# Token step and first inverse step on eight small PE tiles, W fetched once, front reordered

## The chip, the core and the metric

The kernel runs on one core of a Trainium2 chip. The metric is device microseconds of one execution. The engines are PE (TensorE; its weight loads are shown apart as PEld), VectorE (DVE), ScalarE (ACT), GpSimd (POOL) and SyncE (SP), which issues nearly all DMAs.

## The reference

A spectral filter `a` and a diagonal state-space model `b` work on the same `x` (2048 tokens x 1024 features, bf16), and a gate mixes them per token.

```python
X = rfft2(x); X = X * (w_r + 1j * w_i); a = irfft2(X)       # over tokens and features
Lam_bar = exp(dt * Lam)
Bu = x @ B_bar.T                                            # complex, 1024 states
h[t] = Lam_bar * h[t-1] + Bu[t]                             # 2048 steps
b = 2 * real(h @ C.T) + x * Dskip
g = sigmoid((x * gate_w).sum(-1))
out = g * a + (1 - g) * b
```

## The kernel before

**Two strands.** The model strand works through eight chunks of 256 tokens. `unit(c, q)` makes Bu for one chunk and half of the states: two halves (real, imaginary) of 32 matmuls each (L319), with a ScalarE eviction each (L321). `recur` cuts the recurrence of the chunk into pieces for VectorE: products with tables of cosine and sine (L274, L277), joins, scans (L289), and the way back. `early(tb)` multiplies a tile of 128 tokens of h by C (L598, L602) for tiles 0 to 9 and parks the result in DRAM; tiles 10 to 15 are finished in the tail by `own_tile`, and `late_tile` fetches the parked ones.

The spectral strand is a 2D transform by matrix products. The feature step `fd` (L359, L362) works on rows of tokens turned by PE (`turn_x`, L684) and folded by VectorE (`fold`). Then come the first token step `s1` (L376, two tiles of 64 rows side by side), a turn through DRAM (`turn1_dram`, written at L383), the second token step `s2` (L488, a 32-point transform), the product with W (`times_w`, L496 and L497), the first inverse step `is1` (L512, L513, 64-point), a second turn through DRAM, the second inverse step `is2` (L537), and in the tail the inverse feature step (`spectral`, L629).

**s2, product and is1 before.** There are 16 groups of two columns `b`. For a group, `s2` runs two matmuls of 128x128 weights over 512 columns; the 128 rows of weights hold a block structure in which half of the entries are zero (two interleaved 32-point transforms). Its output rows hold real parts in the upper 64 and imaginary parts in the lower 64, so each half of the partitions needs the same W: it is fetched twice, with four DMAs for a group.

```python
for r in range(2):
    nc.sync.dma_start(out=Wb[g % 3][64 * r:64 * (r + 1), w, :, 1:K], in_=W_v[w][:, bs, 1:K])
```

`times_w` makes two products, X2 with the imaginary and with the real part of W. `is1` adds two matmuls of 128x128 weights for each of the two columns. The buffers `psA` are two PSUM tiles of 128x1024 FP32 that all spectral steps share; `psU` has two more, for the model strand.

**Order.** PE, VectorE and ScalarE run in the order in which the program is written; the DMAs of SP and POOL are placed by the framework's scheduler. In the front (until `tctx.close()`), a table `plan` says for each of 16 rows in which order `turn_x` (T), `fold` (f), `fd` (F) and `s1` (S) are issued, and `order` which loads follow: B by DMA transposes (`load_B`, L218), C (`load_C`, L583), tables. Small vectors for the recurrence (L869 to L903) stand in one run after row 5. The tables of cosine and sine (`make_tab`) and halves of the model strand fill in between. After the front the spectral strand is a generator, `gfnet`, which `step()` moves on; between its steps stand halves of the model strand (`halves(ssm, 1)`) and pieces of VectorE's work. `vector(next(share))` issues pieces up to an amount of estimated microseconds from the list `SHARE`.

Group g+3 of `s2`'s input is loaded after `is1` of group g; the 16 groups have one half of the model strand each.

Of the kernel before, what the change touches and what calls it, by code (L numbers as in the profile page):

```python
# [19 lines left out]
S = 2048  # L20
D = 1024
# [24 lines left out]
def _host_consts():  # L46
# [14 lines left out]
    for cls in range(2):  # L61
        for kb in range(2):
# [10 lines left out]
    m1 = np.arange(64)[None, None, :]  # L73
# [8 lines left out]
    f = np.arange(P)  # L82
    fs, fr, fa = f[:, None] // 4, (f[:, None] // 2) % 2, f[:, None] % 2
    hr, hm, ha = f[None, :] // 64, (f[None, :] // 2) % 32, f[None, :] % 2
    angF = 2 * np.pi * ((fs * hm) % 32) / 32
    K2 = (fa == ha) * np.where(fr == hr, np.cos(angF), np.where(fr == 1, 1.0, -1.0) * np.sin(angF))
    pp = (np.arange(P) % 64)[:, None, None]
    bb = np.arange(32)[None, :, None]
    nn = np.arange(64)[None, None, :]
    angM = 2 * np.pi * (((32 * pp + bb) * nn) % S) / S  # L90
    top = (np.arange(P) < 64)[:, None, None]
    Mre = np.where(top, np.cos(angM), -np.sin(angM))
    Mim = np.where(top, np.sin(angM), np.cos(angM))
    gr, gb, ga = f // 64, (f // 2) % 32, f % 2
    angR = 2 * np.pi * ((gb[:, None] * gb[None, :]) % 32) / 32
    R2 = (ga[:, None] == ga[None, :]) * np.where(gr[:, None] == gr[None, :], np.cos(angR),
                                                  np.where(gr[:, None] == 0, 1.0, -1.0) * np.sin(angR))
    R2 = R2.reshape(P, 64, 2).transpose(0, 2, 1).reshape(P, P)
    Sel = np.zeros((P, 2, 2, P))
    for h in range(2):  # L100
        for ri in range(2):
            Sel[2 * np.arange(64) + h, h, ri, 64 * ri + np.arange(64)] = 1.0
# [11 lines left out]
        MT=b16(np.concatenate([-Mim, Mre, Mim], axis=2)),  # L114
        KRS=b16(np.concatenate([K2, R2, Sel.reshape(P, 4 * P)], axis=1)),
# [5 lines left out]
def kernel(  # L121
# [29 lines left out]
    W_v = [w.rearrange("(p b) k -> p b k", b=32) for w in (A_w_r, A_w_i)]  # L151
# [27 lines left out]
    psX = xctx.enter_context(tc.tile_pool(name="psX", bufs=2, space=PSUM, reuse_waits="tile"))  # L179
# [85 lines left out]
    def recur(c, js, home):  # L265
# [21 lines left out]
        def scan(ri, j):  # L287
            seg = u[:, ri, j:j + 4].rearrange("p j t -> p (j t)")
            nc.vector.tensor_tensor_scan(out=seg, data0=rz[:, js.start + j:js.start + j + 4].rearrange("p j t -> p (j t)"),  # L289
                                         data1=seg, initial=0.0, op0=ALU.mult, op1=ALU.add)  # L290
# [14 lines left out]
        t = 0.15 + 0.27 * n  # L305
        both = lambda f, g: lambda: (f(), g())
        pieces = [(t, lambda: cross(1)), (t, lambda: along(0)), (t / 2 + 0.1, join_re), (t / 2 + 0.3, join_im)]
        pieces += [(2.3, lambda ri=ri, j=j: scan(ri, j)) for j in range(0, n, 4) for ri in range(2)]
# [40 lines left out]
    def gfnet():  # L349
# [4 lines left out]
        def fd(j):  # L354
# [9 lines left out]
            X1 = gta.tile([P, 2, K], BF16, name="X1")  # L364
            (nc.vector.tensor_copy if j in (3, 5) else nc.scalar.copy)(  # L365
# [4 lines left out]
        def s1(j):  # L370
# [10 lines left out]
            (nc.vector.tensor_copy if j in (0, 1, 2, 3, 5, 6, 7) else nc.scalar.copy)(out=A1, in_=psa)  # L381
# [14 lines left out]
        MT_sb = raw.rearrange("p (b n) -> p b n", n=192)  # L396
# [5 lines left out]
        t1_v = turn1_dram.rearrange("j (r a b) k -> (j r a) b k", r=2, a=2)  # L402
        Wb = fft["Wb"]

        def load(g):
            bs = slice(2 * g, 2 * g + 2)
            Bb = gt.tile([P, 2, K], BF16, name="Bb", tag="gin", bufs=3)
            nc.sync.dma_start(out=Bb, in_=t1_v[:, bs])
            for w in range(2):
                for r in range(2):  # L410
                    nc.sync.dma_start(out=Wb[g % 3][64 * r:64 * (r + 1), w, :, 1:K], in_=W_v[w][:, bs, 1:K])  # L411
            return Bb

# [22 lines left out]
        loads = [load(0), load(1), load(2)]  # L436
# [4 lines left out]
        nc.vector.tensor_copy(out=Bcol[:, 0:2].rearrange("j c a b -> j (c a b)"), in_=aps)  # L441
# [34 lines left out]
        qps = psA.tile([P, 2, 16], FP32, name="qps", tag="ps")  # L476
        for h in range(2):
            for ri in range(2):
                nc.tensor.matmul(qps[:, h, :], lhsT=fft["Sel"][:, 2 * h + ri, :], rhs=Qb[:, :, ri],
                                 start=(ri == 0), stop=(ri == 1))  # L480
        Qn = fx.tile([P, 2, 16], BF16, name="Qn")
        nc.vector.tensor_copy(out=Qn, in_=qps)
        Qn = Qn.rearrange("p h b -> p (h b)")

        def s2(g):
            ps2 = psA.tile([P, 2, K], FP32, name="ps_s2", tag="ps")
            for h in range(2):
                nc.tensor.matmul(ps2[:, h, :], lhsT=KRS_sb[:, 0, :], rhs=loads[g][:, h, :], start=True, stop=True)  # L488
            X2 = gt.tile([P, 2, K], BF16, name="X2", tag="gev", bufs=3)
            nc.scalar.copy(out=X2, in_=ps2)  # L490
            nc.scalar.copy(out=X2[:, :, 0], in_=Qn[:, 2 * g:2 * g + 2])
            return X2

        def times_w(g, X2):
            V2 = gt.tile([P, 2, K], BF16, name="V2", tag="gv2", bufs=2)
            nc.vector.tensor_mul(out=V2, in0=X2, in1=Wb[g % 3][:, 1])  # L496
            nc.vector.tensor_mul(out=X2, in0=X2, in1=Wb[g % 3][:, 0])  # L497
            return X2, V2

        yield "qn"  # L500
        X2s = [s2(0)]
        yield "s2"
        X2s.append(s2(1))
        UV = times_w(0, X2s.pop(0))
        yield "uv"
        for g in range(16):
            if g + 2 < 16:
                X2s.append(s2(g + 2))
            psc = psA.tile([P, 2, K], FP32, name="ps_is1", tag="ps")
            for h in range(2):  # L510
                b = 2 * g + h
                nc.tensor.matmul(psc[:, h, :], lhsT=MT_sb[:, b, 64:192], rhs=UV[0][:, h, :], start=True, stop=False)  # L512
                nc.tensor.matmul(psc[:, h, :], lhsT=MT_sb[:, b, 0:128], rhs=UV[1][:, h, :], start=False, stop=True)  # L513
            C1 = gt.tile([P, 2, K], BF16, name="C1", tag="gc1", bufs=2)
            nc.scalar.copy(out=C1.rearrange("p h (c i) -> p h c i", c=2), in_=psc.rearrange("p h (i c) -> p h c i", c=2))  # L515
            nc.sync.dma_start(out=turn2_dram[2 * g:2 * g + 2].rearrange("b m k -> m b k"), in_=C1)
            yield "is1"
            if g + 1 < 16:
                UV = times_w(g + 1, X2s.pop(0))
            if g + 3 < 16:  # L520
                loads.append(load(g + 3))
            yield "uv"
        yield "ib"
        ZT = fft["ZT"].rearrange("p i t (h u) -> p i (t h) u", h=2)
        t2_v = turn2_dram.rearrange("b (r G a g) k -> G r b a g k", r=2, a=2, g=4)

        for G in range(8):
            Cq = raw[:, 2 * D * (G % 3):2 * D * (G % 3 + 1)].rearrange("p (g k) -> p g k", g=4)
            for r in range(2):
                nc.sync.dma_start(out=Cq[64 * r:64 * (r + 1)], in_=t2_v[G, r])  # L530
            for kp in range(2):
                psz = psA.tile([P, 2, K], FP32, name="ps_is2", tag="ps")
                for kl in range(2):
                    kc = 2 * kp + kl
                    pv = psz[:, kl, :].rearrange("p (a g n) -> p a g n", a=2, g=4)
                    for g in range(4):
                        nc.tensor.matmul(pv[:, :, g, :], lhsT=Cq[:, g, P * kc:P * (kc + 1)], rhs=KRS_sb[:, 1, :],  # L537
                                         start=True, stop=True)
                nc.scalar.copy(out=ZT[:, 4 * kp:4 * kp + 4, :, 8 * G:8 * G + 8].rearrange("p (c r) n t -> p c r n t", c=2),  # L539
                               in_=psz.rearrange("p c (t r n) -> p c r n t", t=8, r=2))  # L540
                yield "is2"

    def after_ia():
# [10 lines left out]
        fft["Sel"] = fft["gt"].tile([P, 4, P], BF16, name="Sel_sb", tag="gc1", bufs=2)  # L554
        nc.sync.dma_start(out=fft["Sel"], in_=cKRS.rearrange("p (i m) -> p i m", m=P)[:, 2:6])
        fft["Wb"] = [fft["wp"].tile([P, 2, 2, K], BF16, name=f"Wb{i}") for i in range(3)]
# [203 lines left out]
    fft["KRS"] = fx.tile([P, 2, P], BF16, name="KRS_sb")  # L760

    def load_small():
        nc.sync.dma_start(out=fft["JP"], in_=cJP)
        nc.sync.dma_start(out=fft["KRS"], in_=cKRS.rearrange("p (i m) -> p i m", m=P)[:, 0:2])
# [26 lines left out]
    def halves(gen, n):  # L791
# [5 lines left out]
    order = {  # L797
        1: [(load_B, 4)],
        2: [(load_B, 2)],
# [65 lines left out]
    for _ in range(5):  # L865
        front()
# [145 lines left out]
```

## Time and profile before

| | |
|---|---|
| median of 3 runs | 337.9 us (337.06 to 338.51) |
| profiled execution | 338.71 us, span 336.9 us |
| mean granted clock of PE | 0.995 |
| PE busy | 323.7 us (96%), 2446 matmuls |
| VectorE busy | 286.7 us (85%) |
| ScalarE busy | 169.3 us (50%) |
| DMA | 58.45 MB, mean 173 GB/s |
| first matmul of s2, last of s2 | 122.7 us, 191.0 us |
| first matmul of is2 | 211.7 us |

A busy time is the union of an engine's instructions; matmuls overlap, so their mean length (379 ns for 512 columns) is more than the time each holds the engine. Times inside the span count from its start.

### The profile page before, as it was taken

How to read it: one execution, taken by the hardware profiler on the slowest of the kernel's cores; microseconds unless marked ns; L12 is line 12 of the kernel's file. 1: busy time of each engine (PE TensorE's matmuls, PEld its weight loads, DVE VectorE, ACT ScalarE, POOL GpSimd, SP SyncE). 2: the span in 40 equal slices, each digit the busy share in tenths (PEclk: the TensorE clock that was granted, in tenths of full speed). 3: DMA queues.
4: the chain of work that ended last, by engine and by line, in shares of the span. 5: the costliest groups of instructions: out<-in, count | busy, mean ns of one | idle time of the engine just before them, and what ended most of it. 6: DMA issues, size and time to landing. Idle time of an engine off the chain costs nothing.

```text
span 336.9 us, 6192 instructions
## 1 busy us (share of the span) xinstructions
PE 323.7 (96%) x2446; PEld 213.7 (63%) x2446; DVE 286.7 (85%) x403; ACT 169.3 (50%) x213; POOL 32.4 (10%) x64
## 2 busy tenths in 40 slices
PE   8998859999999999999999999999999999999995
PEld 4564636676885675747566576869845876565552
DVE  2798895899979789999999999899680999999951
ACT  3888679746351155647556551646632243443510
POOL 1481112020000000000000000000000002211220
PEclk9999989999999999999999999999999999999999
DMA  7999999999992447889999956997214003776594
GB/s 265 378 175 227 204 211 208 164 172 218 272 220 55 115 135 175 251 192 284 261 253 252 232 163 170 216 195 203 70 28 136 19 0 53 109 159 89 98 156 154
DMA packets 83581, 58.45 MB, mean 173 GB/s; under 512 B 54328, under 2 KB 74304, under 8 KB 83424
## 3 DMA queue, kind: packets, MB, share of 16 engines
q1 hardware_dynamic: 80304, 55.38, 66.8%
q0 software_dynamic: 3168, 2.66, 8.7%
q8 instruction: 19, 0.31, 0.4%
q14 instruction: 10, 0.08, 0.1%
q10 hardware_dynamic: 80, 0.01, 0.0%
HBM read 30.23 MB, written 17.83 MB: 143 GB/s over the span
## 4 chain that ended last, share of the span: by engine, by line
PE 83%; ACT 5%; DVE 5%; SPq 4%; issue 1%; DMA 1%; ACTq 0%; DVEq 0%
PE ps_y L598 29%; PE psu L319 28%; PE ps_h L598 4%; PE ps_id L629 4%; SPq L583 3%; PE ps_fd L359 2%; PE ps_is L537 2%; PE ps_is L513 2%; PE ps_is L512 2%; PE ps_s L488 2%; PE ps_y L602 2%; PE pt L684 2%; PE psw L710 1%; ACT xQ L685 1%; SPq L411 1%
## 5 line engine op out<-in xcount | busy, mean ns | idle before, releaser
L319 PE MATMUL psu<-xQ,BT 128*128 128x256 bf16 x1024 | 117.9, 275 | 0.8 <-ACT ye L616 0.5
L319 PEld LDWEIGHTS <-BT 128*128 128x128 bf16 x1024 | 100.1, 99 | 17.4 <-issue 3.2
L598 PE MATMUL ps_y<-CT,h 128*128 128x512 bf16 x448 | 101.3, 379 | 0.0
L598 PEld LDWEIGHTS <-h 128*128 128x128 bf16 x512 | 49.4, 98 | 55.4
L289 DVE TENSOR_TENSOR_SCAN h<-rz,h 128x1024 bf16<-128x1024 f32 x32 | 71.5, 2274 | 0.1
L321 ACT CAST h<-psu 128x1024 bf16<-128x1024 f32 x32 | 32.3, 1010 | 52.5 <-PE psu L319 49.2
L277 DVE TENSOR_TENSOR h<-h,tab 128x4096 bf16<-128x4096 bf16 (+1 forms) x20 | 37.3, 1863 | 0.7
L644 POOL DMA_DIRECT2D BT<-y_scratch x10 | 11.9, 1194 | 235.4 <-DVE BT L638 235.1
L616 ACT ACTIVATE ye<-ps_y,omg 128x512 f32<-128x512 f32 x20 | 12.7, 684 | 43.4 <-PE ps_y L602 35.7
L274 DVE TENSOR_TENSOR xQ<-h,tab 128x4096 bf16<-128x4096 bf16 x12 | 27.4, 2287 | 4.4 <-ACT h L321 4.3
L490 ACT CAST X<-ps_s 128x1024 bf16<-128x1024 f32 x16 | 16.2, 1014 | 8.7 <-PE ps_s L488 8.7
L359 PE MATMUL ps_fd<-G_sb,preT 128*128 128x512 bf16 x64 | 16.5, 380 | 1.2 <-ACT X L365 1.2
L685 ACT COPY xQ<-pt 128x1024 bf16<-128x1024 bf16 x16 | 15.4, 1024 | 2.5 <-PE pt L684 2.5
L539 ACT CAST ZT<-ps_is 128x1024 bf16<-128x1024 f32 x16 | 15.5, 1023 | 2.2 <-PE ps_is L537 2.2
L695 DVE TENSOR_TENSOR preT<-xQ 128x512 bf16<-128x512 bf16 x16 | 7.3, 453 | 10.9 <-ACT xQ L685 7.6
L515 ACT CAST C<-ps_is 128x1024 bf16<-128x1024 f32 x16 | 16.1, 1008 | 0.0
L629 PE MATMUL ps_id<-raw,ZT 128*128 128x256 bf16 x128 | 15.9, 273 | 0.0
L365 ACT CAST X<-ps_fd 128x1024 bf16<-128x1024 f32 x14 | 14.2, 1013 | 3.0 <-PE ps_fd L362 2.9
L376 PE MATMUL ps_s<-X,raw 64*128 64x512 bf16 x64 | 9.7, 380 | 5.1 <-DVE CT L381 4.5
L598 PE MATMUL ps_h<-CT,h 128*128 128x512 bf16 x64 | 14.5, 379 | 0.0
L629 PEld LDWEIGHTS <-ZT 128*128 128x128 bf16 x128 | 12.4, 98 | 2.2
L496 DVE TENSOR_TENSOR V<-X,Wb 128x1024 bf16<-128x1024 bf16 x16 | 10.9, 680 | 1.6 <-issue 1.5
(194 smaller groups left out, 367.9 us busy)
## 6 DMA issues: line engine op xcount, KB each, us to landing
y_scratch<-ye SPq DMA_DIRECT2D x20, 256.0 KB, 2.6
CT<-in_A_x_dram SPq DMA_DIRECT2D x8, 512.0 KB, 5.4
Bb<-turn_scratch SPq DMA_DIRECT2D x16, 256.0 KB, 4.0
turn_scratch<-C SPq DMA_DIRECT2D x16, 256.0 KB, 5.1
raw<-turn_scratch SPq DMA_DIRECT2D x16, 256.0 KB, 4.5
Wb<-in_A_w_r_dram SPq DMA_DIRECT2D x32, 127.8 KB, 4.1
Wb<-in_A_w_i_dram SPq DMA_DIRECT2D x32, 127.8 KB, 3.8
out_dram<-BT SPq DMA_DIRECT2D x14, 256.0 KB, 5.2
```

Source lines behind the costliest of these rows:

```text
L274: nc.vector.tensor_mul(out=tmps["s"], in0=u[:, ::-1], in1=bc(i))
L277: nc.vector.tensor_mul(out=u, in0=u, in1=bc(i))
L289: nc.vector.tensor_tensor_scan(out=seg, data0=rz[:, js.start + j:js.start + j + 4].rearrange("p j t -> p (j t)"), data1=seg, initial=0.0, ...
L319: nc.tensor.matmul(psu[:, j, :], lhsT=BT[4 * q + j][:, ri, d8, :], rhs=xQ[:, c, d8, :], start=(d8 == 0), stop=(d8 == 7))
L321: nc.scalar.copy(out=hs[c][:, ri, 4 * q:4 * q + 4].rearrange("p b (q j) -> p b q j", j=32), in_=psu.rearrange("p b (j q) -> p b q j", j=32))
L359: nc.tensor.matmul(ps[:, 1, :], lhsT=preTs[j][:, 4 + d4, :], rhs=Go[:, d4, :], start=(d4 == 0), stop=(d4 == 3))
L490: nc.scalar.copy(out=X2, in_=ps2)
L515: nc.scalar.copy(out=C1.rearrange("p h (c i) -> p h c i", c=2), in_=psc.rearrange("p h (i c) -> p h c i", c=2))
L539: nc.scalar.copy(out=ZT[:, 4 * kp:4 * kp + 4, :, 8 * G:8 * G + 8].rearrange("p (c r) n t -> p c r n t", c=2), in_=psz.rearrange("p c (t r ...
L598: nc.tensor.matmul(psy, lhsT=hs[c][:, ri, jb, P * tq:P * (tq + 1)], rhs=CT[ri][:, jb, 512 * dh:512 * (dh + 1)], start=(i == 0), stop=False)
L629: nc.tensor.matmul(pse[:, slot, :], lhsT=ZT_t[:, i, tb, :], rhs=fft["Gi"][:, i, :], start=(kb == 0), stop=(kb == 1))
L685: nc.scalar.copy(out=x_gjq[:, :, :, :, j, :].rearrange("p c d g q -> p d c g q"), in_=pt.rearrange("p d (c q g) -> p d c g q", c=NCH, g=2))
```

## The change

The two steps use tiles of the PE array that are as large as their blocks. `s2` has 8 groups; a group holds two sets of 64 rows (b) and four columns (c), and for the real and the imaginary output (r) it issues eight matmuls of 64 rows by 32 columns. So real and imaginary parts lie side by side in the free dimension, and all 128 partitions hold different values of the token index. `is1` has four accumulating passes of eight matmuls of 32 rows by 64 columns. W is fetched once, for four columns at a time and two groups (`load_W`; two buffers, one of them in `raw`, where the smaller table `MT` leaves room). A product takes both parts of W at once, with X2 spread over the two parts of W and W spread over the two parts of X2.

```diff
+        def load_W(i):
+            pair, w = i // 2, i % 2
+            for c in range(4):
+                nc.sync.dma_start(out=Wb[pair % 2][32 * c:32 * (c + 1), w, :, 1:K], in_=W_v[w][c][:, 4 * pair:4 * pair + 4, 1:K])
...
         def s2(g):
-            ps2 = psA.tile([P, 2, K], FP32, name="ps_s2", tag="ps")
-            for h in range(2):
-                nc.tensor.matmul(ps2[:, h, :], lhsT=KRS_sb[:, 0, :], rhs=loads[g][:, h, :], start=True, stop=True)
-            X2 = gt.tile([P, 2, K], BF16, name="X2", tag="gev", bufs=3)
-            nc.scalar.copy(out=X2, in_=ps2)
-            nc.scalar.copy(out=X2[:, :, 0], in_=Qn[:, 2 * g:2 * g + 2])
+            ps2 = [psA.tile([P, 2, K], FP32, name="ps_s2", tag="ps") for _ in range(2)]
+            for r in range(2):
+                for c in range(4):
+                    for b in range(2):
+                        nc.tensor.matmul(ps2[b][32 * c:32 * (c + 1), r, :], lhsT=KRS_sb[64 * b:64 * (b + 1), 0, 32 * r:32 * (r + 1)],
+                                         rhs=loads[g][64 * b:64 * (b + 1), c, :], start=True, stop=True, tile_position=(64 * b, 32 * c))
+            X2 = []
+            for b in range(2):
+                X2.append(gt.tile([P, 2, K], BF16, name="X2", tag="gev", bufs=2))
+                nc.scalar.copy(out=X2[b], in_=ps2[b])
+                nc.scalar.copy(out=X2[b][:, :, 0], in_=Qn[:, 2 * g + b, :])
...
-            nc.vector.tensor_mul(out=V2, in0=X2, in1=Wb[g % 3][:, 1])
-            nc.vector.tensor_mul(out=X2, in0=X2, in1=Wb[g % 3][:, 0])
+                nc.vector.tensor_mul(out=UV[b], in0=X2[b].unsqueeze(1).to_broadcast([P, 2, 2, K]),
+                                     in1=Wb[g // 2 % 2][:, :, at:at + 1, :].to_broadcast([P, 2, 2, K]))
...
-                nc.tensor.matmul(psc[:, h, :], lhsT=MT_sb[:, b, 64:192], rhs=UV[0][:, h, :], start=True, stop=False)
-                nc.tensor.matmul(psc[:, h, :], lhsT=MT_sb[:, b, 0:128], rhs=UV[1][:, h, :], start=False, stop=True)
+            psc = [psA.tile([P, 2, K], FP32, name="ps_is1", tag="ps") for _ in range(2)]
+            for i, (u, r, n) in enumerate(((0, 0, 64), (0, 1, 32), (1, 0, 32), (1, 1, 0))):
+                for c in range(4):
+                    rows = slice(32 * c, 32 * (c + 1))
+                    for b in range(2):
+                        nc.tensor.matmul(psc[c // 2][64 * b:64 * (b + 1), c % 2, :], lhsT=MT_sb[rows, 2 * g + b, n:n + 64],
+                                         rhs=UV[b][rows, u, r, :], start=(i == 0), stop=(i == 3), tile_position=(32 * c, 64 * b))
```

The reads and writes of the two turns through DRAM follow the new index order (the read for `is2` is one DMA for a group instead of two); `is2` keeps its 128 matmuls of 128x128. `qps` is one matmul instead of four.

The order of the whole program up to the tail is now one string, `ORDER`, with a letter for each act: T, f, F, S as above, h a half of the model strand, v a share of VectorE's pieces, t a part of a cosine table, a a part of the small vectors (now the generator `small`), b one B transpose, c a part of C, s a step of the spectral strand, w and k loads, g the gate.

```diff
+ORDER = (
+    "FTfSTbTTFSbfTbfbTTFfTTSfbbFbTbfbTwSTSFf2TTbaFfSabaxatfbbFbhtSttt",
+    "fFftbbSthttFShStttfthfFkttFtvttthtStvgfFcFtStShtvtcvttchtttSFtth",
+    "tttvFcSttttSt|cvvcsccdhvhvvehvshhvshhvvshvhvshvsshvshvsshvshvssh",
+    "vsvhshsvshvsshshvsvshvshvsshvsvhsshvshvshvhvhvsvshvsvshvsvshsvvs",
+    "hvsvvshsvshvsivshvsvsvh",
+)
-    psX = xctx.enter_context(tc.tile_pool(name="psX", bufs=2, space=PSUM, reuse_waits="tile"))
+    psX = xctx.enter_context(tc.tile_pool(name="psX", bufs=4, space=PSUM, reuse_waits="tile"))
-        pieces += [(2.3, lambda ri=ri, j=j: scan(ri, j)) for j in range(0, n, 4) for ri in range(2)]
+        pieces += [(2.3 * m / 4, lambda ri=ri, j=j: scan(ri, j, m)) for j in range(0, n, m) for ri in range(2)]
-            X1 = gta.tile([P, 2, K], BF16, name="X1")
-            (nc.vector.tensor_copy if j in (3, 5) else nc.scalar.copy)(
+            X1 = gta.tile([P, 2, K], BF16, name="X1", bufs=4)
+            (nc.vector.tensor_copy if j in (0, 3, 5, 10, 15) else nc.scalar.copy)(
-            (nc.vector.tensor_copy if j in (0, 1, 2, 3, 5, 6, 7) else nc.scalar.copy)(out=A1, in_=psa)
+            (nc.vector.tensor_copy if j in (0, 1, 3, 5, 6, 9) else nc.scalar.copy)(out=A1, in_=psa)
```

In `ORDER`, `s2` of a group and `is1` of the group before alternate, with one half of the model strand between each two. Of the eight c, four stand in the front, two before the step `w` (which issues the first loads of `s2`'s input and of W), and two after it. `SHARE` has new values; up to the last half ahead of the tail they sum to 160.7 in place of 154.6. A scan now runs over all eight blocks of a chunk at once where `recur` has the whole chunk.

More of the change, by code (lines that the diff above doesn't have):

```diff
@@ L435, in gfnet @@
         nc.vector.tensor_scalar_mul(out=beta, in0=beta, scalar1=0.25)
-        loads = [load(0), load(1), load(2)]
+        loads = [load(0), load(1)]
+        for i in range(4):
+            load_W(i)
         yield "w"
@@ L475, in gfnet @@
         yield "q"
[L476 to L483, printed above, removed]
-        def s2(g):
-            ps2 = psA.tile([P, 2, K], FP32, name="ps_s2", tag="ps")
-            for h in range(2):
-                nc.tensor.matmul(ps2[:, h, :], lhsT=KRS_sb[:, 0, :], rhs=loads[g][:, h, :], start=True, stop=True)
-            X2 = gt.tile([P, 2, K], BF16, name="X2", tag="gev", bufs=3)
-            nc.scalar.copy(out=X2, in_=ps2)
-            nc.scalar.copy(out=X2[:, :, 0], in_=Qn[:, 2 * g:2 * g + 2])
+        qps = psA.tile([P, 32], FP32, name="qps", tag="ps")
@@ new lines, in gfnet @@
+        nc.tensor.matmul(qps, lhsT=KRS_sb[:, 2, :], rhs=Qb.rearrange("p b r -> p (b r)"), start=True, stop=True)
+        Qn = fx.tile([P, 16, 2], BF16, name="Qn")
+        nc.vector.tensor_copy(out=Qn.rearrange("p b r -> p (b r)"), in_=qps)
+        def s2(g):
+            ps2 = [psA.tile([P, 2, K], FP32, name="ps_s2", tag="ps") for _ in range(2)]
[9 more added lines that the diff above has]
+                nc.scalar.copy(out=X2[b][:, :, 0], in_=Qn[:, 2 * g + b, :])
@@ L876 @@
-    xctx.close()
-    pools["u"] = ctx.enter_context(tc.tile_pool(name="psU", bufs=2, space=PSUM, reuse_waits="tile"))
-    for _ in turns:
-        pass
     sth, cth = s2c[:, 0], c2c[:, 0]
-    sTC = sp.tile([P, 8], FP32, name="sTC"); nc.vector.tensor_mul(out=sTC, in0=s2c[:, 1], in1=r_sb)
-    cTC = sp.tile([P, 8], FP32, name="cTC"); nc.vector.tensor_mul(out=cTC, in0=c2c[:, 1], in1=r_sb)
+    sTC = sp.tile([P, 8], FP32, name="sTC")
+    cTC = sp.tile([P, 8], FP32, name="cTC")
     rot = sp.tile([P, 2, 2, 8], FP32, name="rot")
-    nc.vector.tensor_copy(out=rot[:, 0, 1], in_=sTC)
@@ L917 @@
-    tctx.close()
-    for q in range(4, 8):
-        load_C(q)
-    for v, n in (("w", 4), ("a", 1), ("z", 2), ("q", 2), ("qn", 1), ("s2", 0), ("uv", 1)):
-        assert step() == v
-        for i in range(n):
-            if v == "w" and i == 0:
-                nc.vector.tensor_mul(out=fft["dgD"], in0=ident.unsqueeze(1).to_broadcast([P, 8, P]),
-                                     in1=vecT[:, 3].unsqueeze(2).to_broadcast([P, 8, P]))
-            if v == "w" and i == 3:
-                gate_end()
-            halves(ssm, 1)
-            vector(next(share))
@@ L930 @@
-    for g in range(16):
-        assert step() == "is1"
-        assert step() == "uv"
-        halves(ssm, 1)
-        vector(next(share))
-    halves(ssm, 1)
-    vector(next(share))
-    halves(ssm, 1)
-    vector(next(share))
-    for g in range(16):
-        assert step() == "is2"
-        if g == 12:
-            after_ic()
-        if g % 2:
-            halves(ssm, 1)
-        vector(next(share))
+    lbr = sp.tile([P, 8], FP32, name="lbr")
+    lbi = sp.tile([P, 8], FP32, name="lbi")
+    nr = sp.tile([P, 8], FP32, name="nr")
@@ new lines, with turn, use_psU, front_done @@
+    tables = chain(*(make_tab(jp) for jp in range(4)))
+    smalls = small()
+    turns_left = [14]
+    def turn(r):
+        turn_x(r)
+        turns_left[0] -= 1
+    def use_psU():
+        assert not turns_left[0]
+        xctx.close()
+        pools["u"] = ctx.enter_context(tc.tile_pool(name="psU", bufs=2, space=PSUM, reuse_waits="tile"))
+    def front_done():
+        for _ in tables:
+            pass
+        tctx.close()
+    def make_dgD():
+        nc.vector.tensor_mul(out=fft["dgD"], in0=ident.unsqueeze(1).to_broadcast([P, 8, P]),
+                             in1=vecT[:, 3].unsqueeze(2).to_broadcast([P, 8, P]))
```

248 lines of the change are left out of this document (112 added, 136 removed), and 10 rows, old and new, of the table SHARE.

## The prediction

> **What bounds the kernel now.** I read the page first: busy shares, then the chain of waits by engine.
>
> ```profile
> PE 323.7 (96%) x2446; PEld 213.7 (63%) x2446; DVE 286.7 (85%) x403; ACT 169.3 (50%) x213; POOL 32.4 (10%) x64
> ...
> PE 83%; ACT 5%; DVE 5%; SPq 4%; issue 1%; DMA 1%; ACTq 0%; DVEq 0%
> ```
>
> PE is nearly never idle, and it is the chain. So a change pays if it takes matmul time out of a stretch where PE is packed, or closes a gap of PE; all else must only stay hidden. Next, busy time by stretch (columns: length, then PE, PEld, DVE, ACT, POOL with counts, clock, DMA share, GB/s), to see where the gaps are.
>
> ```profile
> 10.00:20.00 10.00, 9.14 (x98) 5.88 (x96) 7.90 (x18) 8.86 (x12) 5.53 (x20) 1.00 1.18 316
> 20.00:30.00 10.00, 8.66 (x85) 5.49 (x85) 9.83 (x23) 9.38 (x12) 6.21 (x12) 1.00 1.20 192
> 30.00:40.00 10.00, 8.88 (x70) 6.12 (x70) 7.20 (x32) 6.48 (x12) 1.22 (x2) 1.00 1.00 225
> 40.00:50.00 10.00, 6.60 (x46) 4.55 (x44) 9.82 (x22) 7.34 (x12) 1.44 (x2) 0.88 1.18 217
> ...
> 80.00:90.00 10.00, 8.98 (x89) 6.79 (x88) 9.76 (x18) 4.47 (x6) 0.00 (x0) 1.00 0.93 236
> ```
>
> ```profile
> 121.00:204.00 83.00, 83.00 (x545) 51.77 (x543) 80.38 (x74) 46.83 (x65) 0.00 (x0) 1.00 0.85 219
> 204.00:260.00 56.00, 55.47 (x475) 39.67 (x474) 42.48 (x29) 26.02 (x31) 0.00 (x0) 1.00 0.60 142
> ```
>
> The front loses 0.86 + 1.34 + 1.12 + 3.40 + 1.02 = 7.7 us of PE in these five stretches. From 86 us on PE is packed, but VectorE is at 97% in 121 to 204, where the second token step (L488) and first inverse step (L512, L513) lie; it has 13.5 us free in 204 to 260. The waits of PE name the largest front gap: PE waits for a VectorE eviction.
>
> ```profile
> PE ps_s L376 <- DVE CT L381: 4.5, 2, 3.4
> ```
>
> **The eight tiles.** What is removed, from the groups by form and the chain:
>
> ```profile
> L512 PE MATMUL ps_is<-X,raw 128*128 128x512 bf16 x32 | 12.1, 379 | 0.0
> L497 DVE TENSOR_TENSOR X<-X,Wb 128x1024 bf16<-128x1024 bf16 x16 | 11.1, 692 | 0.6
> L496 DVE TENSOR_TENSOR V<-X,Wb 128x1024 bf16<-128x1024 bf16 x16 | 10.9, 680 | 1.6 <-issue 1.5
> L277 DVE TENSOR_TENSOR h<-h,tab 128x2048 bf16<-128x2048 bf16 x8 | 9.8, 1224 | 0.3
> L488 PE MATMUL ps_s<-Bb,KRS_sb 128*128 128x512 bf16 x32 | 9.4, 379 | 0.0
> ```
>
> ```profile
> 85.47 0.38 PE Wrev_ps L420 x15
> ...
> 190.97 0.43 PE ps_s L488 x2
> 191.40 0.22 PE ps_is L512
> ```
>
> A 512-column matmul lasts 0.379 us alone but holds the chain for 0.216 (0.43 for two). So the old steps hold it for (32 + 64) x 0.216 = 20.7 us.
>
> The new ones issue 128 matmuls of 64x32 tiles and 256 of 32x64, all 512 columns. If eight tiles run as one round, that is 16 + 32 = 48 rounds. No row shows eight at once; the nearest are four column tiles (the gate, L737) and two row tiles (L376), in the timeline (start, length, then group):
>
> ```profile
> 62.99 0.60 PE L319 MATMUL psu<-xQ,BT 128*128 128x256 bf16 x4
> 63.52 1.91 PE L737 MATMUL zps_g<-xQ,gw 128*32 128x512 bf16 x32
> 65.36 0.60 PE L359 MATMUL ps_fd<-G_sb,preT 128*128 128x512 bf16 x2
> ...
> 71.67 0.60 PE L362 MATMUL ps_fd<-G_sb,preT 128*128 128x256 bf16 x4
> 72.20 0.60 PE L376 MATMUL ps_s<-X,raw 64*128 64x512 bf16 x4
> 72.74 0.39 PE L319 MATMUL psu<-xQ,BT 128*128 128x256 bf16 x2
> ```
>
> The gate's 32 matmuls hold PE from 63.52 to 65.36, 1.84 us: eight rounds at 0.216 (1.73) and 0.11 more. Four tiles side by side cost what one costs. L376's two rounds of two take 0.54, again 0.43 and 0.11. That 0.11 is a change of tile shape on leaving; entering costs 0.09 (four L362 of 0.109 take 0.53 instead of 0.44). The rest of the kernel stays 128x128, so each of the 16 bursts (8 of each step) pays 0.20 for both changes: 3.3 us. Sum: 48 x 0.216 + 3.3 = 13.7, a saving of 7.0; I take 6.9 for the staggered starts.
>
> Instruction supply: L420 passes a load and a matmul each 0.38 / 15 = 0.025 us, so eight pairs need 0.20, under 0.216. That is close, but only 16 to 32 pairs come in a row, and 3.5 us of wide matmuls stand ahead of each burst.
>
> Bounds per round: 0.216 (as the gate) and 8 x 0.097 = 0.78 (weight loads, 92 to 97 ns each at L737, end to end). I take the low end, the nearer row: L737 has eight loads per two rounds and still keeps 0.216.
>
> L737's 32 loads run under matmuls that use the same 128 rows, so I let none of them show. The Trainium skill (TensorE: Matmul & The Clock Gate, Part 3, The mechanism) says that a weight load overlaps matmuls in flight only when its row group differs; by that rule the loads would show between the rounds, as in the third rival below. The trace disagrees at L737.
>
> **Hand-overs.** Both steps now take both `psA` buffers at once, and each waits for ScalarE to empty the other's. Between them stands one half unit (3.49 us of L319, or 3.67 of L598 and L602). After s2 ScalarE has perhaps 1.0 left of the half's eviction, then 1.01 + 0.1 + 1.01 + 0.1 (L490, L491): some 3.4 us after s2's start, and is1 starts 0.65 + 3.49 = 4.1 after it. Cover 0.7, so I book nothing; the bound is 0 to 0.5 us at each of 15. `X2` has one pair of buffers, so this eviction also waits for VectorE's product of the group before; VectorE may lag PE by some 1.7 us before ScalarE feels it, and behind the waiting eviction on ScalarE stand the half's eviction and then PE.
>
> **VectorE.** 32 products (22.0 us) become 16 of twice the size; L277's 128x2048 row with one spread input says 1.22 each, 19.6. Bounds 1.22 to 2.45 (no row has both inputs spread). Half-scans joined in pairs: about nothing (L289 is 2.27 per 1024). Three more X1 evictions and one fewer A1: +2.4. From first product to last, VectorE then has 46 of recurrence pieces (SHARE) and 19.6, 66 us; PE has 16 halves and 14 us of bursts, 70. It fits.
>
> The new SHARE puts 6 us more pieces ahead of the late tiles (160.7 against 154.6 up to there). VectorE had ended there at 251.3 and idled to 260.9, so this fits too and lightens the tail, where chunk 7 was done at 315.8 for a tile that began at 317.6. The tail is otherwise unchanged.
>
> **DMA.** W issues on SP halve, 64 to 32 at 0.60 us; W lands three groups (some 26 us) ahead of its products. One of four tiny matmuls of `qps` stays and its own table load goes: nothing. The first loads grow from 15 to 20 issues (+3 us of SP), MT shrinks from 1.5 to 0.5 MB, and s2 is ten halves (36 us) later: hidden. Two C parts (four transposes, 1.3 us each) now stand behind these loads; the second half of early tile 0, some 19 us on, needs them. Behind 20 issues and with 4 to 7 us of landing they would cost 0 to 5 us. SP issued C (60.5 to 73.1) ahead of W (76.4 on) before, so I take 0.
>
> **The front.** Same matmuls; the tables, the 26 small VectorE steps with ScalarE's 1.28 us table switch among them, the B transposes on SP (now one at a time) and the evictions are spread otherwise, with four `psX` and four X1 buffers. POOL's fetch of W's columns and the gate's two moves shift too; their users are tens of us later. Gain: at most the 7.7 us of gaps. Against it: X1 of row 15 moves to VectorE behind 18.5 us of pieces, and SP was issuing almost without a pause from 9 to 88 us; a wait of `s1` for VectorE, or of A1's four slots for SP, can stand in for the old one. VectorE also has 2.4 us more. Bounds: +2 (slower) to -7.7; I take half of the gaps, -4.0, because the 3.4 us wait comes from the order of VectorE's work alone (A1 of row 7 behind two folds), and that order goes.
>
> **Sum.** The profiled execution took 338.71 (336.9 of span, 1.8 around it), 0.8 above the median. 338.7 - 6.9 - 4.0 = 327.8, or 327.0 on the median's scale.
>
> **Rivals** (on that scale).
> - The front gives nothing: 338.7 - 6.9 - 0.8 = 331.0. For it: SP's full queue, DMA share about 1. Against: 6.7 of the 7.7 us lie before 50 us, where VectorE's order is at fault.
> - The front gives all: 323.3.
> - The loads of a round wait for the round before: 32 inner rounds (8 + 24) lose 0.097 each, 3.1 us: 330.1. Against: L737's pitch.
> - A round is not one pass, so the tiles don't do what they are for. At two passes (0.432) the bursts take 24.0, +3.3: 338.7 + 3.3 - 4 - 0.8 = 337.2. At 0.78, 40.7: 354. It turns slower from (20.7 + 4 - 3.3) / 48 = 0.45 us per round. Against: rows and columns each overlap fully.
> - Slower: the product with both inputs spread costs 2.45. VectorE needs 46 + 39 = 85 against PE's 70, each is1 waits for it, and 15 us come back: 338.7 - 10.9 + 15 - 0.8 = 342. It decides from (70 + 10.9 - 46) / 16 = 2.2 us per product. Against: L277 at 2048 elements keeps the rate of the 1024 ones.
>
> **How the numbers follow.** Forecast 0.50, front gives nothing 0.18, front gives all 0.10, waiting loads 0.04, no single pass 0.10 (half about even, half slower), costly product 0.08. A measurement can tell 0.5% (1.7 us) from no change. Faster 0.82, same 0.05, slower 0.13. The range 321.5 to 335 holds the first four but for their outer edges: the front's full gain and 1 to 2 us more below, the front's nothing with a few us of hand-over or C waits above.
>
> **What would show it.** Right: the group of each new step has eight matmuls per 0.22 us; bursts 0.65 (s2) and 1.08 (is1) long in the chain; product 1.2 to 1.3; PE without idle from the first `w` step to the tail; PE idle in 10 to 50 us down from 6.7 to about 3. Wrong: rounds over 0.3 us, PE waiting for X2 or UV, `s1` of row 15 waiting for VectorE, early tile 0 waiting for CT.

## The result and the profile after

The changed kernel took 335.93 us (median of 20 executions, 330.45 to 340.2 and one of 411 at a mean clock of 0.755), the kernel before 338.52 (337.06 to 339.35). The ratio is 0.9832, 95% interval 0.9805 to 0.9858; it counts only executions near each kernel's fastest, and since the spread of this kernel is itself part of the story, I compare medians of all executions below. In a later series the same kernel took 335.65 (333.85 to 339.60, ratio 0.9907, 0.9877 to 0.9938). So it is faster than before, by 2.6 to 3.2 us of the medians; the forecast was 327.0 with a range up to 335.0. The profiled execution took 335.79, 333.8 of span.

The page of the changed kernel, busy shares and the chain by engine:

```profile
PE 317.1 (95%) x2731; PEld 207.7 (62%) x2731; DVE 286.3 (86%) x377; ACT 167.4 (50%) x211; POOL 32.5 (10%) x62
...
PE 79%; DVE 9%; ACT 7%; issue 2%; DMA 1%; ACTq 0%
```

PE lost 6.6 us of busy time, and the chain holds more of the other engines than before. The new steps, by form (times executed, then busy time and mean ns):

```profile
L503 DVE TENSOR_TENSOR UV<-X,raw 128x2048 bf16<-128x2048 bf16 x8 | 9.4, 1218 | 5.4 <-PE ps_is L513 3.3 <-ACT h L320 2.1
...
L513 PE MATMUL ps_is<-UV,raw 32*64 32x512 bf16 x256 | 8.6, 380 | 0.0
...
L489 PE MATMUL ps_s<-Bb,KRS_sb 64*32 64x512 bf16 x128 | 5.0, 381 | 0.0
```

The product costs 1.218 us, and 256 and 128 matmuls cost 8.6 and 5.0 us. In the timeline (start, length, group), one burst of each:

```profile
148.44 0.63 PE L489 MATMUL ps_s<-Bb,KRS_sb 64*32 64x512 bf16 x16
149.00 3.63 PE L611 MATMUL ps_y<-CT,h 128*128 128x512 bf16 x16
152.47 0.39 PE L615 MATMUL ps_y<-dgD,xs 128*128 128x128 bf16 x4
152.78 1.07 PE L513 MATMUL ps_is<-UV,raw 32*64 32x512 bf16 x32
153.78 3.67 PE L318 MATMUL psu<-xQ,BT 128*128 128x256 bf16 x32
```

Sixteen matmuls in two rounds, 32 in four. From the end of the last full-size matmul's turn (the time for which it holds PE) to the first of the next, a burst takes 0.651 us (second step) and 1.095 (inverse step): 0.09 at the entry, 0.216 for a round, 0.01 to 0.02 more for the first round, and 0.12 at the exit. Eight bursts of each make 13.97 us, against 20.71 before.

Now by stretch (length, then PE, PEld, DVE, ACT, POOL with counts, clock, DMA share, GB/s):

```profile
40.00:50.00 10.00, 9.59 (x82) 7.15 (x80) 8.16 (x23) 8.60 (x14) 1.29 (x2) 1.00 1.18 229
60.00:70.00 10.00, 7.73 (x75) 4.49 (x75) 9.79 (x13) 7.51 (x10) 1.15 (x1) 1.00 1.10 204
80.00:90.00 10.00, 5.94 (x51) 3.64 (x50) 8.08 (x16) 3.02 (x3) 0.00 (x0) 0.88 0.98 263
87.70:91.10 3.40, 3.40 (x18) 2.44 (x17) 2.96 (x11) 0.27 (x1) 0.00 (x0) 0.50 1.11 244
121.00:204.00 83.00, 83.00 (x883) 50.81 (x881) 75.23 (x54) 48.31 (x66) 0.00 (x0) 1.00 0.68 187
```

The hole at 40 to 50 us is closed (6.60 of PE before, 9.59 now). In its place PE misses 2.3 us at 60 to 70, and 4.1 us at 80 to 90, right ahead of the step `w`. From 87.7 us on stands a stretch of 3.4 us at clock 0.50, worth 1.7 us; before had one at 47.7 to 51.1:

```profile
47.70:51.10 3.40, 3.40 (x18) 2.42 (x17) 3.29 (x10) 2.08 (x5) 0.00 (x0) 0.50 1.41 133
```

What PE waits for now, and the chain at 80 to 87 us (start, length, what):

```profile
PE Wrev_ps L419 <- ACT A L380: 3.3, 1, 3.3
PE ps_s L375 <- DVE CT L380: 1.9, 2, 1.1
```

```profile
77.12 3.51 PE psu L318 x32
80.63 0.02 issue
80.65 0.64 ACT h L320
81.28 4.58 DMA turn_scratch<-A
...
85.96 1.02 ACT A L380
86.98 0.14 issue
87.12 0.16 PE Wrev_ps L419
```

The wait for VectorE fell from 4.5 to 1.9 us, but a new one of 3.3 came. (The view counts a wait from the modelled end of the last matmul. Counted from the end of its turn, 0.16 us earlier, this gap of PE is 3.44; the gaps below are counted so.) A1 of row 14 takes the place of row 10 among four; the write of row 10 to DRAM was issued at 81.28 only and landed 4.58 later; ScalarE then evicted row 14, and PE's `Wrev_ps` needed that PSUM buffer. SP's queue shows why it was issued so late, first in the changed kernel, then in the one before:

```profile
72.44 8.12 SPq L596 DMA_TRANSPOSE CT<-in_B_C_re_dram  x5
80.67 0.52 SPq L396 DMA_DIRECT2D raw<-c_MT  x1
81.28 0.38 SPq L382 DMA_DIRECT2D turn_scratch<-A  x1
```

```profile
85.93 1.06 SPq L383 DMA_DIRECT2D turn_scratch<-A  x2
87.08 0.45 SPq L397 DMA_DIRECT2D raw<-c_MT  x1
87.63 0.68 SPq L383 DMA_DIRECT2D turn_scratch<-A  x1
```

It stood behind the C transposes, and MT's load now goes ahead of it. Before, MT filled all of T2's memory and came behind all A1 writes but the last; a third of the size needs only T2's first part, can be loaded early, and was put ahead of the writes of rows 10 to 15.

### The profile page after: what moved, and what is told of

Read it like the earlier page. It is cut to its first block, busy times and chain, and to the rows that moved or that the text cites. A ratio compares the mean times of both kernels' runs of the same rounds, so it can differ in the third digit from the quotient of the medians.

```text
span 333.8 us, 6647 instructions
## 1 busy us (share of the span) xinstructions
PE 317.1 (95%) x2731; PEld 207.7 (62%) x2731; DVE 286.3 (86%) x377; ACT 167.4 (50%) x211; POOL 32.5 (10%) x62
## 4 chain that ended last, share of the span: by engine, by line
PE 79%; DVE 9%; ACT 7%; issue 2%; DMA 1%; ACTq 0%
PE ps_y L611 29%; PE psu L318 29%; PE ps_h L611 4%; PE ps_id L642 4%; PE ps_is L513 2%; PE ps_is L551 2%; PE ps_y L615 2%; PE ps_fd L358 1%; DMA turn_scratch<-A 1%; PE ps_s L489 1%; ACT h L320 1%; ACT X L364 1%; PE psw L723 1%; DVE X L364 1%; DVE CT L380 1%
## 5 line engine op out<-in xcount | busy, mean ns | idle before, releaser
L287 DVE TENSOR_TENSOR_SCAN h<-rz,h 128x2048 bf16<-128x2048 f32 (+1 forms) x20 | 70.9, 3563 | 0.2
L517 ACT CAST C<-ps_is 128x1024 bf16<-128x1024 f32 x16 | 15.4, 1019 | 0.0
L503 DVE TENSOR_TENSOR UV<-X,raw 128x2048 bf16<-128x2048 bf16 x8 | 9.4, 1218 | 5.4 <-PE ps_is L513 3.3
L380 ACT CAST A<-ps_s 128x1024 bf16<-128x1024 f32 x7 | 7.1, 1018 | 9.8 <-DVE h L275 5.5
```

## The experiments

All kernels in one table; the ratios are made like the one above, to runs of the kernel before in the same series (its median there was 338.5 to 338.9). Each changed kernel has 4 to 20 executions, of which one is profiled; the 411 us are left out of the range. "w" is the start of the step `w` in the profiled execution, "behind" the time from there to the end of the last matmul.

| kernel | median us (range) | ratio to before | w | behind |
|---|---|---|---|---|
| before | 338.52 (337.06 to 339.35) | 1 | 85.3 | 248.06 |
| changed, first | 335.93 (330.45 to 340.2) | 0.983 (0.981 to 0.986) | 87.1 | 243.07 |
| changed, again | 335.65 (333.85 to 339.60) | 0.991 (0.988 to 0.994) | 85.5 | 243.07 |
| tiles, old front | 335.24 (334.15 to 337.86) | 0.991 (0.988 to 0.994) | 87.3 | 241.40 |
| new front, old steps | 342.54 (341.19 to 347.13) | 1.011 (1.008 to 1.015) | 83.7 | 252.30 |
| writes on POOL | 331.33 (331.05 to 331.42) | 0.978 (0.976 to 0.980) | 84.3 | 241.42 |
| own memory for late A1 | 330.82 (330.35 to 330.93) | 0.976 (0.974 to 0.978) | 83.3 | 241.41 |
| W's part late | 335.96 (333.66 to 337.86) | 0.991 (0.988 to 0.995) | 85.6 | 242.85 |
| MT late | 332.40 (330.42 to 335.40) | 0.980 (0.978 to 0.983) | 86.7 | 243.06 |
| MT and W late | 330.93 (330.74 to 334.69) | 0.981 (0.977 to 0.985) | 83.9 | 241.41 |
| before, wait filled | 337.31 (336.49 to 339.95) | 0.996 (0.993 to 0.998) | 84.1 | 248.06 |
| tiles, old front, own memory | 332.34 (331.63 to 332.52) | 0.981 (0.979 to 0.982) | 85.2 | 241.40 |
| and row 7 on ScalarE | 329.43 (329.20 to 329.55) | 0.973 (0.971 to 0.974) | 82.4 | 241.40 |
| and row 9, steps moved | 335.79 (334.79 to 336.00) | 0.990 (0.988 to 0.992) | 89.1 | 241.40 |

**1. Tiles behind the old front.** Everything up to the step `w` as before (order, buffers, engines of the evictions), the new steps behind it.

```
-    "FTfSTbTTFSbf ... tSt|cvvcsccdhvh ...",      (ORDER, up to the step w)
+    "FTfSTfTFTfTS ... tttv|ccccsdhvh ...",
-    psX: bufs=4; X1: bufs=4; evictions by VectorE: X1 of rows 0, 3, 5, 10, 15, A1 of rows 0, 1, 3, 5, 6, 9
+    psX: bufs=2; X1: bufs=2; evictions by VectorE: X1 of rows 3, 5, A1 of rows 0, 1, 2, 3, 5, 6, 7
```

> The eight tiles, the big product and W fetched once, behind the front of before (its order, its two X1 and two psX buffers, its choice of engines for the evictions). Theory A: the tiles bring their 6.7 us whatever stands ahead of them, and what is missing in the result was given back by the new front. Then this kernel takes 338.5 - 6.7 = 331.8 us (331 to 333), the first matmul of the step w starts near 85.3 us as before, and the stretch from there to the last matmul is 241 to 242 us. Theory B: the new front did gain, and the new steps lose it again later (hand-overs, VectorE, the clock). Then the time is 336 to 340 us, and the stretch behind the step w is 245 us or more.

Measured 335.24: behind `w` exactly the gain of the tiles (241.40 against 248.06, 6.66 us), but `w` starts at 87.3 instead of 85.3, behind a wait for A1 of 2.0 us (0.4 before). The stretch at half clock that goes with the wait at 43 us is longer here, 6.8 us (44.9 to 51.8) in place of 3.4. So theory A is right behind `w`, and wrong ahead of it: the late write isn't a matter of the new order, it comes with the new steps, even behind the old front.

**2. The new front alone**, with the steps of before (and their MT of 1.5 MB).

> The new front alone, with the second token step, the product, the first inverse step, W and the constants of before behind it. Theory A: the front alone costs time. Its step w starts 1.8 us later than before's, and before's start holds a stretch at half clock (1.7 us) that the new front has only behind it: 338.5 + 1.8 + 1.7 = 342.0 us (340 to 344). Theory B: the front gains the 4.0 us that were forecast: 334.5 us (332 to 336).

342.54 is theory A's number, but not by its mechanism. `w` started at 83.7 us, with no wait for A1 at all; 252.30 us behind it are 4.2 more than before, of which two waits for VectorE make 3.9. That the old steps' shares of VectorE's work don't fit behind this front is the likely reason; no run tries it.

```profile
PE ps_h L606 <- DVE h L309: 2.3, 1, 2.3
PE ps_y L606 <- DVE h L309: 1.6, 1, 1.6
```

These two waits are absent before and after. So this run says nothing of the front's worth but that it starts `w` 1.6 us sooner, no more than the missing stretch at half clock (1.7), and that with the old MT and W there is no late write.

**3 and 4. Taking the write's wait away in two ways**: by another queue, and by memory of its own (rows 12 to 14 in the half of `raw` that T2 leaves free, row 15 in the place of row 8).

```
-            nc.sync.dma_start(out=t1_w[j], in_=A1)
+            (nc.gpsimd if j >= 8 else nc.sync).dma_start(out=t1_w[j], in_=A1)
```

```
-            A1 = ... if j < 8 else A1_4[:, j % 4]
+            A1 = ... if j < 8 else A1_own[j]
+    A1_own[12 + i] = raw[:, (3 + i) * D:(4 + i) * D]   # i = 0, 1, 2
```

> The changed kernel with one difference: the writes of A1 of rows 8 to 15 are issued on POOL's queue and not on SP's. Theory A: PE's last gap of the front (3.44 us ahead of the step w) stands because row 14 takes the A1 buffer of row 10, whose write SP issued at 81.3 us, 13 us or more after it was ready, behind eight C transposes. Then ScalarE's wait for this write (4.3 us) is below 1 us, step w starts near 84 us, and the time is 3 to 5 us under that of the changed kernel: 331 to 333 us. Theory B: the write is late for its own length or for the memory, not for SP's queue: the wait stays at 3 us or more, and the time within 1 us of 335.9.

> The changed kernel with one difference: A1 of rows 12 to 14 has memory of its own, and row 15 takes the place of row 8, so that no late row waits for a late write; SP's queue is as it was. Theory A: ScalarE's wait for the write is gone, step w starts near 84 us, and the time is 331 to 333 us, as with the writes on the other queue. Theory C: the wait is real but not alone; VectorE's recurrence pieces ahead of the keeping of A1's columns (5.5 us of wait in the changed kernel) or the loads of the second token step behind SP's queue take its place: step w starts at 86 us or later, and the time is 335 to 336 us.

331.33 and 330.82, both as theory A said, and the spread fell from ten microseconds to 0.4 and 0.6 (five and four executions). In one point the second run's edit does more than its text says: rows 12 to 14 lie where the second buffer of W is, so W's early loads can no longer come at 60 us. Experiment 6 shows that this alone gains nothing. With own memory, the only wait of PE at 70 to 95 us and the stretch:

```profile
PE ps_s L375 <- DVE X L364: 0.8, 1, 0.8
```

```profile
80.00:90.00 10.00, 9.22 (x92) 7.05 (x90) 9.15 (x20) 4.05 (x4) 0.12 (x1) 1.00 1.02 298
```

PE 9.22 instead of 5.94, clock 1.00 instead of 0.88. The late write and the clock's stretch behind it cost 5 us of the median, and with them most of the spread goes.

**5. The changed kernel again.**

> The changed kernel once more, unaltered, for a second profile and beside the next three on the same chip. Theory A: its time goes with the gap ahead of the step w, which differs from run to run (B transposes on SP ended at 50.1 us in the first profile): single runs from 330.5 (no gap, clock 1.0) to 340 us, and in this profile the gap and the lateness of SP's queue at 50 us go together. Theory B: the gap is the same in each run, and the spread comes from elsewhere.

334.20 in the profiled execution; gap 2.25 us instead of 3.44, `w` at 85.5. SP had finished the B transposes at 45.4 us instead of 50.1. The gap does differ between executions with SP's lateness, but even with SP about as early as in the kernels that keep these writes on SP and have no gap (44.1 us in experiment 2, 44.4 in 4, 45.5 in 8), more than 2 us were left. The mean clock recorded for each of the 19 first executions shows how the spread is made: 330.5 to 332.6 us at 0.998 to 1.000, 333.3 to 335.8 at 0.994 or 0.995, 336.1 to 339.4 at 0.989 or 0.990, 340.2 at 0.985. One stretch at half clock is worth 0.005 (the profiled execution had one and 0.994), so each step down is most likely one more of them; where they lay, no trace shows.

```profile
PE Wrev_ps L419 <- ACT A L380: 2.1, 1, 2.1
```

**6. W's part held back, 7. MT held back, 8. both.** Four loads of W's second buffer stood at 60.6 us among the C transposes; MT ahead of row 10's write.

```
         keep_A1(12)
+        nc.gpsimd.tensor_copy(out=raw[:, 0:1], in_=A1_4[:, 3, 0, 0:1])                     # MT
+        nc.gpsimd.tensor_copy(out=raw[:, 4 * D:6 * D] ...[:, :, 1], in_=A1_4[:, 3, 0, 0:4])  # W
```

> The changed kernel with one difference: the imaginary half of the second buffer of W can't be loaded before A1 of row 15 is there (a copy of four elements per partition on POOL from that A1 into the buffer). In the changed kernel SP issues these four loads at 60.6 us, between the C transposes, for 2.0 us. Theory A: they are a part of SP's lateness: the C transposes and the late A1 writes are issued 2 us earlier, the gap ahead of the step w falls by about 2 us, and the time by 2 to 4: 332 to 334 us. Theory B: the pace of the transposes alone decides: the time stays at 335 to 336 us.

> The changed kernel with one difference: the load of MT (0.5 MB) can't start before A1 of row 15 is there (a copy of one element per partition on POOL from that A1 into MT's place). In the changed kernel MT, now a third of its size, needs only the first part of the table T2's memory, and SP issues it right ahead of the write of A1 of row 10; in the kernel before it came behind all but one of these writes. Theory A: this load is what makes the write of row 10 late, by its own issue (0.5 us) and by its bytes in the queue (the write landed 6.4 to 6.7 us after its issue behind MT, 3.4 to 4.7 elsewhere): the gap ahead of the step w falls below 1 us in most runs, and the time to 331 to 332.5 us with little spread. Theory B: SP's lateness behind the C transposes alone decides: the gap falls by the 0.5 us of the issue, the time stays at 334.5 to 336 us.

> The changed kernel with both loads held back until A1 of row 15 is there: MT and the imaginary half of W's second buffer, so that no load of the new steps stands ahead of the write of row 10. Theory A: with 2.5 us less of issues and MT's bytes gone, the write lands before ScalarE asks for its place: no gap ahead of the step w, step w at 83.4 to 84 us, 330.5 to 331.5 us, as with memory of its own. Theory B: as in the run before, 334 us or more.

W alone: 335.96, nothing. The write of row 10 was issued at 77.67 us, 0.8 sooner than in experiment 5, and landed 6.7 us later, behind MT's bytes; the gap was 1.9 us. MT alone: 332.40, 3.3 us less than the unaltered kernel, but from 330.42 to 335.40, not with the little spread of theory A. Both: 330.93, four of six executions within 0.4 us of each other, the other two at 333.8 and 334.7. SP's queue, first in experiment 5, then with both held back:

```profile
77.86 0.52 SPq L396 DMA_DIRECT2D raw<-c_MT  x1
78.47 0.38 SPq L382 DMA_DIRECT2D turn_scratch<-A  x1
```

```profile
73.67 4.41 SPq L598 DMA_TRANSPOSE CT<-in_B_C_re_dram  x3
78.59 0.37 SPq L382 DMA_DIRECT2D turn_scratch<-A  x1
...
86.58 0.40 SPq L382 DMA_DIRECT2D turn_scratch<-A  x1
87.12 0.46 SPq L398 DMA_DIRECT2D raw<-c_MT  x1
```

The write of row 10 was issued at 78.47 and at 78.59 us. The same time, with MT behind it instead of ahead: ScalarE, which waited for it, could evict row 14 at 82.72 instead of 84.38, and there was no gap instead of 2.25 us. So in that execution of the changed kernel MT's bytes in the queue made the write late, and not the time of its issue. In its first profile it was mostly the issue: 81.28 us, and 4.58 to landing. What remains is SP's own lateness: the execution of "MT late" that was profiled, the slowest of six, had its B transposes finished at 49.7 us, issued the write at 82.60, and still had a gap of 2.9. Why the B transposes take 5 us more in some executions of the same program stays open; the writes wait for them in any case, and only own memory or another queue makes the kernel indifferent to it.

**9. The kernel before with its 3.57 us gap (a wait of 3.4 in the view) filled** by 14 matmuls of no use.

```
-    8: 'FfS'
+    8: 'FfKS'      # K: 14 matmuls of ident by 512 columns of BT[0] into an idle PSUM buffer
```

> The kernel before with one addition: 14 matmuls of 0.216 us whose result nobody reads, in PE's 3.57 us wait for VectorE at 43.2 us. They fill the wait and nothing else. Theory A: the stretch at half clock (47.7 to 51.1 us) follows from this wait; filled, it is gone, and the kernel takes 338.5 - 1.7 = 336.8 us. So 1.7 of the front's length was clock and not waiting. Theory B: the clock falls for another reason, or the wait itself is what costs: 338.5 us as before.

337.31 against 338.88 beside it: 1.6 us less, with more work. The stretch at half clock is gone:

```profile
40.00:50.00 10.00, 9.56 (x69) 6.33 (x68) 9.83 (x22) 7.32 (x12) 1.44 (x2) 1.00 1.09 197
```

Clock 1.00 instead of 0.88. So 1.7 us of the old front was clock and not waiting. The Trainium skill (TensorE: Matmul & The Clock Gate, Part 1: The HAM clock gate) says that PE goes to half rate after an idle window of about 3.4 us which runs free of the program. The traces agree on the length and the rate (3.4 us at 0.50, twice that in experiments 1 and 12), and on the free window: each stretch of full clock that lies inside a trace is a whole number of 3.413 us (40.96, 81.92 and 286.72 us are 12, 24 and 84). But the window need not be idle throughout. Laid on this grid, the eight falls of the clock each follow a window in which PE idled between 2.05 us (experiment 1) and 3.41 (experiment 12), and no window at full clock with 1.84 us or less brought one. So it counts where a gap lies in the grid, and that differs between executions: a gap of 2.25 us inside one window brought half clock in experiment 5, while one of 2.19 in experiment 1 brought none, as the grid cut it at 85.9 us into 0.6 and 1.4 of idle time.

**10. Old front with tiles and own memory, 11. and A1 of row 7 on ScalarE.**

```
-            (nc.vector.tensor_copy if j in (0, 1, 2, 3, 5, 6, 7) else nc.scalar.copy)(out=A1, in_=psa)
+            (nc.vector.tensor_copy if j in (0, 1, 2, 3, 5, 6) else nc.scalar.copy)(out=A1, in_=psa)
```

> The eight tiles behind the old front, as in the first experiment, with memory of its own for A1 of rows 12 to 14 (row 15 in the place of row 8). Theory A: the gap ahead of the step w (2.0 us) goes and its stretch at half clock too, the 3.57 us wait at 43 us with its stretch stays: 335.2 - 2.0 - 1.7 = 331.5 us (330.5 to 332.5), so that the two fronts, once neither waits for the late writes, differ by under 1 us. Theory B: the new front is better by some us in itself: 333.5 us or more here, against 330.8 for the new front with the same memory.

> The eight tiles behind the old front with own memory for late A1 (332.3 us), with one difference: A1 of row 7 is evicted by ScalarE and not by VectorE, where it stood behind two folds and made PE wait 3.4 us at 43 us. It tries the reason that the prediction gave for half of the front's gaps: that this wait comes from VectorE's order alone and goes with it. Theory A: the wait goes whole, and its stretch at half clock with it: 332.3 - 3.4 - 1.7 = 327.2 us (326.5 to 328.5). Theory B: another wait stands right behind it (X1 of the next row on ScalarE, the small steps of the tables there): only 1 to 2 us of the wait and the clock's 1.7 go: 329 to 330 us.

332.34: the two fronts differ by 1.5 us once neither waits for the late write, and that is the stretch at half clock, which the old front has and the new one hasn't. Theory A's time, though not by its terms: experiment 1 had no stretch behind the late gap, but the one at 45 us was 6.8 us long there and is 3.4 here. Then 329.43 with the one eviction moved, 9 us under the kernel before (ratio 0.9726, 0.9713 to 0.9738), the best of all: theory B. The wait that I took for VectorE's order is gone, but half of it came back 10 us later, on ScalarE (waits of PE at 36 to 60 us):

```profile
PE ps_s L375 <- ACT X L364: 1.9, 2, 1.6
PE ps_s L375 <- DVE CT L380: 1.1, 1, 1.1
```

**12. That wait taken away as well**: A1 of row 9 to VectorE, two steps of the tables behind X1 of row 10.

```
-    "...tFfStthttSfFtthtv..."      (ORDER)
+    "...tFfStthSfFtttthtv..."
-    A1 by VectorE: j in (0, 1, 2, 3, 5, 6)
+    A1 by VectorE: j in (0, 1, 2, 3, 5, 6, 9)
```

> The kernel of the run before (eight tiles, old front, own memory for late A1, A1 of row 7 on ScalarE; 329.4 us), with the next wait taken away in the same manner: at 53 us PE waited 1.75 us for X1 of row 10, which stood on ScalarE behind two table steps and A1 of row 9. Here that A1 goes to VectorE, and the two table steps come behind X1 (two letters of the order moved). Theory A: the waits of the front are each an order of one engine and can be taken away one by one while there is room: 329.4 - 1.75 = 327.7 us (327 to 328.3). Theory B: the front stays as long, since the next wait stands right behind, as half of it did when the wait for row 7 went: 328.7 us or more.

335.79, 6 us worse: theory B, and more. The wait at 53 us is gone, and at 58.7 us stands a gap of 6.0, with PE at half clock from 63.2 to 70.0. (The other way, X1 of row 10 evicted by VectorE, has no time: its order ends in a deadlock.) The waits of all engines at 48 to 70 us:

```profile
ACT rot_kk L853 <- DVE ang L851: 5.9, 2, 5.4
PE zps_g L756 <- ACT A L380: 5.8, 1, 5.8
DVE preT L711 <- PE ps_fd L361: 3.5, 1, 3.5
```

Read from the bottom: VectorE's next fold, now ahead of the table steps, waited for PE to free its `preT` buffer; ScalarE's table step waited for VectorE; the A1 eviction queued behind it, and the gate waited for that.

## Why the prediction was wrong, point by point

- **The tiles: right.** Forecast a saving of 6.9 us, measured 6.74 in the bursts and 6.66 behind `w`, the same in seven kernels (241.40 to 241.42). Bursts of 0.65 and 1.08 were forecast, 0.651 and 1.095 measured; the rival of loads that wait for the round before (3.1 us) didn't come. Of the 384 loads, which all lie beside matmuls, at most the 0.01 to 0.02 us of a burst's first round shows, so the Trainium skill's rule on weight loads, which the prediction weighed, doesn't describe this place either.
- **Product, hand-overs, VectorE: right.** 1.218 us for 1.22. From 91 us to the end PE waits as long as before (0.7 us). VectorE has 7.8 us of room in 121 to 204.
- **C parts at nothing: right for the early tiles**, which didn't wait; but the same queue held the A1 writes.
- **DMA, the step that failed first.** "MT shrinks from 1.5 to 0.5 MB, and s2 is ten halves (36 us) later: hidden." The size was counted, not the place: a smaller MT needs less of T2's memory, so SP issues it ahead of six A1 writes. It costs 3.3 us of the median (332.40 against 335.65), and with W's early part 4.7.
- **The front's -4.0, the step that failed second.** The reason, that the 3.4 us wait goes with VectorE's order, was half true. PE's waits ahead of `w` sum to 8.7 us before and 8.6 in the new front without the late write ("MT and W late"): the time reappeared as many small waits (the gate for X1 1.1, `preT`, A1, X1). PE's idle time in 10 to 50 us fell from 6.7 to 4.4 and not to 3, and rose by 2.3 at 60 to 70. The only gain was 1.7 us of clock, which the sum did not have: the rows of before showed it as 0.88 and 0.94 at 40 to 60 us, and I had shown the first of them without asking what it was worth. Experiment 11 shows the same of the old order: `w` came 2.7 us sooner, of which 1.7 is clock, so at most 1.0 of the 3.4 us of wait was gained (PE's listed waits ahead of `w` fell from 8.7 to 8.0).
- **The stand-in** ("a wait of `s1` for VectorE, or of A1's four slots for SP") was named, with 2 us as its bound. It came, as 2 to 3.4 us and 1.7 of clock behind it.
- **The sum as it was**: 338.5 - 6.7 (tiles) - 0.1 (waits) - 1.7 (clock) = 330.0, near the rival "front gives nothing" (331.0) and the 330.8 to 330.9 of the kernels without a late write; the late write and its stretch at half clock then add 5. Some 0.8 are left over, of which the time around the span (1.8 us before, 2.0 to 2.2 in these kernels) is 0.2 to 0.4.

## What to carry to other kernels

When a change shrinks or moves a buffer, ask of every transfer that shares its memory not only how long it takes but from when it may start: an order made by free memory puts it ahead of something that others wait for. A wait of the bounding engine is worth its length only if the trace shows that nothing else is late right behind it; in this front, where four engines take turns, at most a third of such a wait was gained, and as much again or more was clock, so read the granted clock of the stretch beside it. If a kernel's executions spread by some per cent where the old one's don't, look for a wait that hangs on a transfer, and give that transfer a buffer of its own.

## What the runs showed of the hardware

- Eight tiles of 64x32 or 32x64 run as one pass: 0.216 us per round of eight 512-column matmuls (the changed kernel), with some 0.09 us for entering the shape and 0.12 for leaving it; the weight loads of such tiles (0.09 and 0.10 us) all lie beside matmuls.
- A stretch of PE at half clock is 3.4 us long, or 6.8 (experiments 1 and 12); 3.4 us of it cost 1.67 us of packed matmuls (243.07 against 241.40). It followed gaps of 1.9 to 6.0 us, in some executions and not in others, always after a window of 3.413 us with 2.05 us or more of idle PE (experiment 9).
- The same program's transposing loads of B ended at 45.4 us in one execution and at 50.1 in another.
